# A three-layer kernel on one core: the sigmoids of the opening, the decoding of weight parts, and fill products rearranged

## The chip, the cores and the metric

The kernel runs on one NeuronCore of a Trainium2 chip. The metric is the device time of one execution in microseconds; the figure for a kernel is the median of its runs. The core has five engines with queues of their own: TensorE (PE; its weight loads are shown as PEld), VectorE (DVE), ScalarE (ACT), GpSimd (POOL) and SyncE (SP), which here only issues transfers. Each engine takes its instructions strictly in the order in which they were laid down when the kernel was compiled.

## The reference, cut to what matters

Three stages follow one another. The first is a recurrent attention over 768 steps for 2 batches x 8 heads of width 40, with gates i, f and o; the two others are feed-forward layers of 320 to 2048 to 320 with different nonlinearities, over 1536 tokens.

```python
for t in range(S):                                   # first stage, per batch and head
    m_new = np.maximum(f_gate[t] + m, i_gate[t])
    C = exp(f_gate[t] + m - m_new) * C + exp(i_gate[t] - m_new) * outer(v[t], k[t])
    n = exp(f_gate[t] + m - m_new) * n + exp(i_gate[t] - m_new) * k[t]
    y[t] = sigmoid(o_gate[t]) * (C @ q[t]) / max(abs(n @ q[t]), 1.0)
h = x @ w_in;  x = (h - np.tanh(h)) @ w_out          # second stage (layer 1 below)
h = x @ w_in2; x = (h * tanh(softplus(h))) @ w_out2  # third stage (layer 2 below)
```

## The kernel before, in words

**Tokens and weights.** The 1536 tokens are 12 tiles of 128 (`order`: chunk by chunk, both batches of a chunk together). Layer 1 takes them in six blocks of two tiles, layer 2 in three of four. Each layer's weights come as 16 parts (`NF`), each 128 hidden columns with their share of `w_in` and `w_out`. The loaded words are 64-bit numbers.

**Decoding a part** (`conv_w`) turns them into a high and a low 32-bit half: two steps on VectorE (L179, L180), a scaling on ScalarE (L181), another step on VectorE (L182), a copy that rounds to the high half (`copy_r`, L144 on ScalarE, L148 on GpSimd), and two subtractions that give the remainder, the low half (L185, L186). So a part has five steps on VectorE where the remainder is there too. Before, GpSimd does the remainder for parts 0 and 1 of layer 1 (`f < PRE`), and the high copy for the parts of layer 2 that are decoded before that layer begins (`layer and not second`). `load_w` issues the load of the next part; the buffers are three of `rawp` (parts 0 to 2 of layer 1 lie elsewhere), so a load waits until an earlier part is decoded.

**Attention** (`attention(j)`, a generator that is advanced piece by piece) handles one token tile: decay matrix by products and Exp on ScalarE (L300), scores times decay on VectorE (L319), products with the state (`it`, L326) and with the values (`pv`, L337), denominators, multiplication with the sigmoid of the o gate, and the new state. Tiles of chunk 0 need no state from before. `transpose_x` turns a finished token tile (three transposes, a copy on ScalarE, L252, a subtraction on VectorE, L253) into the input x of layer 1.

**The sigmoids.** `session(c0, c1)` runs the sigmoids of these chunks on ScalarE. They need another function table than Exp and Tanh, so each session has two table loads; the second is forced by a dummy Exp on `scr`, which is recorded in `tbl`. Before, there are two sessions: chunks 0 and 1 in the opening, chunks 2 to 5 in block k = 2 of `attend`. `load_o` loads the o gate in three pieces: chunk 0, chunk 1, and the other four (1.28 MB, inside `lead1`).

**Layer 1 and layer 2.** `tiles` lists the work: layer 1 in two phases, parts 0 to 9 over all six blocks, then parts 10 to 15; each tile takes two parts (`mm1`, 16 products of 256 columns; `tile1`, the nonlinearity on ScalarE, VectorE and GpSimd; `mm2`, two tiles later, 12 products of 320 columns). In layer 2 each tile takes one part and four token tiles (`tile2`, with its own table, Mish). `conv_to` and the main loop decide in which tile a part is decoded: `lead1` for layer 1, `lead2` for layer 2. In layer 2 parts are decoded during the first of the three groups of token tiles.

**Order.** `tc.issue_after(x)`, here `with after([...])`, lays an instruction behind x in the queue of x's engine. Within these bounds a planner lays the instructions of each engine in order when the kernel is compiled, by its own estimate of times and by the order in the source. Fill products (`spin`, `fill[0](n)`, `keep(n, x)`) multiply constants into a bank that nobody reads, to keep TensorE at work; `fill.clear()` ends them after the fifth tile.

## Time and profile before

| | us |
|---|---|
| median of three runs | 486.01 |
| lowest, highest | 485.80, 488.79 |
| the profiled execution | 489.08 |
| its span on the core | 487.3 |
| TensorE busy in the span | 464.8 (95%) |
| VectorE, ScalarE, GpSimd busy | 323.5, 277.8, 129.3 |
| mean granted clock of TensorE | 0.965 of full |

The profile shows one execution, 1.8 us longer than its span. Rows of its order of time give start, length, engine, source line, operation, what is written and from what, the shapes, and the count where neighbours are merged. In square brackets stands how long the engine was idle just before, and whose result ended that. A merged row is as long as from its first start to its last end. The ends of matmuls are modelled, and a few of their records can be missing.

### The profile page before, as it was taken

The page shows a single profiled execution, that of the slowest core. Times are in us where ns is not written, and L with a number is a line of the kernel's source. Part 1 is how long each engine was busy: PE and PEld are TensorE (multiplying, and loading weights), DVE is VectorE, ACT ScalarE, POOL GpSimd, SP SyncE. Part 2 cuts the span into 40 slices and gives each one's busy share as a digit, 9 for nine tenths or more (in the row PEclk, how much of TensorE's full clock was granted, in tenths as well). Part 3 has the DMA queues.
Part 4 walks back from the last instruction along what each step waited for, and adds up shares of the span by engine and source line. Part 5 has one row for each costly group of instructions (what it writes and reads, how often), then busy time and mean ns, then how long its engine had stood idle before and what let it go on. Part 6 is the DMA issues. An engine that isn't in the chain of part 4 may idle for free. (4 is left out here: it accounts for less than half of the span.)

```text
span 487.3 us, 8052 instructions
## 1 busy us (share of the span) xinstructions
PE 464.8 (95%) x3107; PEld 421.0 (86%) x3107; DVE 323.5 (66%) x546; ACT 277.8 (57%) x496; POOL 129.3 (27%) x143
## 2 busy tenths in 40 slices
PE   9867999899999999999999889999999999999996
PEld 5645788899999999999998778998899899899895
DVE  6799798669994978757959998779863222122111
ACT  2858346938836667478777666856663333233231
POOL 2733443343735434334442333200000000000000
PEclk9957799859999999999999999999999999999999
DMA  7951563341060421000110111054301000010001
GB/s 255 370 184 63 179 229 94 100 124 65 37 196 10 128 77 59 1 1 2 61 60 1 60 61 60 2 179 165 132 0 55 0 1 2 0 55 0 1 1 54
DMA packets 22886, 38.05 MB, mean 78 GB/s; under 512 B 1504, under 2 KB 17184, under 8 KB 22848
## 3 DMA queue, kind: packets, MB, share of 16 engines
q1 hardware_dynamic: 22848, 37.54, 23.3%
q8 instruction: 24, 0.39, 0.3%
q14 instruction: 14, 0.11, 0.1%
HBM read 35.41 MB, written 1.97 MB: 77 GB/s over the span
## 5 line engine op out<-in xcount | busy, mean ns | idle before, releaser
L491 PE MATMUL h<-xT,w 128*128 128x256 f32 (+1 forms) x1152 | 210.3, 326 | 10.3 <-DVE t L523 4.2
L491 PEld LDWEIGHTS h<-xT,w 128*128 128x128 f32 x1152 | 170.9, 192 | 28.9 <-issue 6.5
L558 PE MATMUL acc<-w,gh 128*128 128x320 f32 x384 | 121.4, 318 | 1.9 <-DVE xo L575 1.8
L559 PE MATMUL acc<-w,gh 128*128 128x320 f32 x384 | 119.6, 313 | 0.0
L560 PE MATMUL acc<-w,gl 128*128 128x320 f32 x384 | 113.9, 313 | 0.0
L510 POOL TENSOR_TENSOR gl<-g,gh 128x512 fp32r<-128x512 f32 x48 | 65.2, 1359 | 95.3 <-ACT gh L144 84.7
L541 DVE TENSOR_TENSOR gl<-g,gh 128x512 fp32r<-128x512 f32 x48 | 33.2, 691 | 86.2 <-ACT g L540 86.0
L558 PEld LDWEIGHTS acc<-w,gh 128*128 128x128 f32 x384 | 73.1, 190 | 6.8 <-issue 3.2
L559 PEld LDWEIGHTS acc<-w,gh 128*128 128x128 f32 x384 | 73.1, 190 | 2.4
L539 ACT ACTIVATE gh<-h 128x512 fp32r<-128x512 f32 x48 | 28.7, 598 | 76.5 <-PE h L491 76.4
L560 PEld LDWEIGHTS acc<-w,gl 128*128 128x128 f32 x384 | 70.7, 190 | 1.2 <-DVE gl L541 0.3
L144 ACT ACTIVATE gh<-g 128x512 fp32r<-128x512 f32 x48 | 30.4, 633 | 27.5 <-DVE g L528 25.0
L528 DVE COPY_PREDICATED g<-u,t 128x512 f32<-128x512 uint32 x48 | 40.5, 849 | 7.1 <-ACT u L527 6.9
L527 ACT ACTIVATE u<-u,bias 128x512 f32<-128x512 f32 x48 | 34.8, 725 | 16.6 <-DVE g L522 16.5
L522 DVE TENSOR_TENSOR g<-u,h 128x512 f32<-128x512 f32 x48 | 32.7, 681 | 16.4 <-ACT u L521 12.2
L181 ACT ACTIVATE raw<-raw 128x704 f32<-128x704 f32 x32 | 27.5, 864 | 18.6 <-DVE raw L180 18.5
L519 ACT ACTIVATE u<-h 128x512 f32<-128x512 f32 x48 | 28.4, 591 | 16.7 <-PE h L491 16.7
L182 DVE SCALAR_TENSOR_TENSOR raw<-raw 128x704 uint32<-128x704 uint32 x32 | 32.2, 1013 | 4.4 <-ACT raw L181 4.3
L523 DVE TENSOR_TENSOR t<-h,t 128x512 f32<-128x512 f32 x48 | 32.8, 683 | 0.0
L180 DVE SCALAR_TENSOR_TENSOR raw<-raw 128x704 uint32<-128x704 uint32 x32 | 31.3, 981 | 0.3
L521 ACT ACTIVATE u<-u 128x512 f32<-128x512 f32 x48 | 30.4, 638 | 0.0
L144 ACT ACTIVATE w<-raw 128x704 fp32r<-128x704 f32 x27 | 23.0, 867 | 12.6 <-DVE raw L182 12.3
(105 smaller groups left out, 518.8 us busy)
## 6 DMA issues: line engine op xcount, KB each, us to landing
raw<-in_w_dram SPq DMA_DIRECT2D x32, 704.0 KB
qk_t<-in_qk_dram SPq DMA_DIRECT2D x12, 512.0 KB
kv_t<-in_kv_dram SPq DMA_DIRECT2D x12, 324.0 KB
out_dram<-xo SPq DMA_DIRECT2D x12, 160.0 KB
xo<-in_og_dram SPq DMA_DIRECT2D x2, 640.0 KB
xo<-in_og_dram SPq DMA_DIRECT2D x2, 320.0 KB
sd<-nr SPq DMA_DIRECT2D x20, 4.0 KB
md<-nr SPq DMA_DIRECT2D x20, 4.0 KB
```

Source lines behind the costliest of these rows:

```text
L144: nc.scalar.activation(out=o, in_=x, func=AF.Copy)
L182: nc.vector.scalar_tensor_tensor(z, in0=z, scalar=3, in1=lo32, op0=ALU.logical_shift_left, op1=ALU.bitwise_or)
L491: y = nc.tensor.matmul(t[:, k * nt:(k + 1) * nt], lhsT=w[:, o:o + P], rhs=x[:, kk, :], start=(n == 0), stop=(n == len(pairs) - 1),)
L510: nc.gpsimd.tensor_tensor(gl, in0=g, in1=gh.bitcast(F32), op=ALU.subtract)
L522: mark[:] = [nc.vector.tensor_tensor(g, in0=u, in1=h, op=ALU.mult)]
L523: nc.vector.tensor_tensor(t, in0=h, in1=t, op=ALU.subtract)
L527: nc.scalar.activation(out=u, in_=u, func=AF.Relu, bias=bias[:, 0:1])
L528: nc.vector.copy_predicated(out=g, mask=u.bitcast(U32), data=t)
L541: nc.vector.tensor_tensor(gl, in0=g, in1=gh.bitcast(F32), op=ALU.subtract)
L558: nc.tensor.matmul(a, lhsT=gh[:, sl], rhs=wh, start=(f in ends_), stop=False)
L559: nc.tensor.matmul(a, lhsT=gh[:, sl], rhs=wl, start=False, stop=False)
L560: nc.tensor.matmul(a, lhsT=gl[:, sl], rhs=wh, start=False, stop=(f + 1 in ends_ or f == NF - 1))
```

## The change

- `session(0, NCH)` in the opening takes the sigmoids of all six chunks; the session in `attend` goes. The third piece of the o gate is loaded in the first series of loads, right behind weight part 1.
- The copies that complete x for chunk 0 are laid behind the sigmoids, the exponential of `rest_t` behind the dummy Exp, weight part 1's decoding behind the sigmoids (`lead1(PRE, sig)`; on ScalarE).
- Weight parts 2 and up to 9 are laid behind the transposes of the first x (`lead1(..., start)`); the gates' last step also behind the high copy of the part before (`cvd`). Tanh of tile i is laid behind the scaling of part 2i + 2, for the first four tiles.
- Part 1's remainder moves from GpSimd to VectorE. All high copies are on ScalarE.
- Fill products follow the products of the first three tiles, not five; four are added behind each of the two transposes of the first x.
- GpSimd's setting of `sd` and `md` is traced before the first decoding, not after the second.
- Layer 2: four parts are decoded before its first tile, every fourth tile of layer 1's second phase (`R2, E2`: 3, 5 to 4, 4); the rest is spread to 6/7 of a part per tile, not 4/5.

```diff
@@ -129,9 +129,9 @@
 
     last, chain, fill, mark, second = [], [], [], [], []
 
-    texp, tbl, dls = [], [], []
-
-    spq = []
+    texp, tbl, dls, sig = [], [], [], []
+
+    spq, cvd = [], []
 
     def after(x):
         e = ExitStack()
@@ -148,8 +148,7 @@
             nc.gpsimd.tensor_scalar(o, in0=x, scalar1=1.0, scalar2=0.0, op0=ALU.mult, op1=ALU.add)
 
 
-    wtile = {}
-    raw = {}
+    wtile, raw, scaled = {}, {}, {}
     ER = 3
     pending_loads = [(l, f) for l in range(2) for f in range(NF)]
 
@@ -178,10 +177,10 @@
 
         nc.vector.tensor_scalar(lo32, in0=lo32, scalar1=29, scalar2=None, op0=ALU.logical_shift_right)
         nc.vector.scalar_tensor_tensor(lo32, in0=z, scalar=0x80000000, in1=lo32, op0=ALU.bitwise_and, op1=ALU.bitwise_or)
-        nc.scalar.activation(out=zf, in_=zf, func=AF.Copy, scale=2.0 ** -111)
+        scaled[layer, f] = nc.scalar.activation(out=zf, in_=zf, func=AF.Copy, scale=2.0 ** -111)
         nc.vector.scalar_tensor_tensor(z, in0=z, scalar=3, in1=lo32, op0=ALU.logical_shift_left, op1=ALU.bitwise_or)
-        copy_r(2 if layer and not second else 0, w[:, 0:WC], zf)
-        eng = nc.gpsimd if layer == 0 and f < PRE else nc.vector
+        cvd[:] = [nc.scalar.activation(out=w[:, 0:WC], in_=zf, func=AF.Copy)]
+        eng = nc.vector if layer or f else nc.gpsimd
         eng.tensor_tensor(w[:, WC:WT], in0=zf[:, 0:REM0], in1=wf[:, 0:REM0], op=ALU.subtract)
         eng.tensor_tensor(w[64:P, REM0:REM1], in0=zf[64:P, REM0:REM1], in1=wf[64:P, REM0:REM1], op=ALU.subtract)
         wtile[layer, f] = w
@@ -353,7 +352,8 @@
         nc.vector.scalar_tensor_tensor(
             x, in0=x, scalar=1 / WS, in1=den.to_broadcast([P, H, D]), op0=ALU.mult, op1=ALU.mult
         )
-        copy_r(0, xo[:, j, DM:3 * P], xo[:, j, 2 * P:DM])
+        with after(() if c else sig):
+            copy_r(0, xo[:, j, DM:3 * P], xo[:, j, 2 * P:DM])
         yield
         if c + 1 < NCH:
             st = at_ps([P, HG, D1], "st")
@@ -445,7 +445,8 @@
             return rest_t
 
         def rest_t():
-            nc.scalar.activation(out=u_t, in_=u_t, func=AF.Exp, scale=-1.0)
+            with after(tbl):
+                nc.scalar.activation(out=u_t, in_=u_t, func=AF.Exp, scale=-1.0)
             u_ps = at_ps([P, NCH, BH], "u_ps")
             for c in range(NCH):
                 nc.tensor.transpose(u_ps[:, c, :], ch(u_t)[:, c, :], ident[0:BH, 0:BH])
@@ -492,7 +493,7 @@
                     t[:, k * nt:(k + 1) * nt], lhsT=w[:, o:o + P], rhs=x[:, kk, :], start=(n == 0),
                     stop=(n == len(pairs) - 1),
                 )
-            if i < F0[1] // NP:
+            if i < 3:
                 keep(3, y)
         hps[i] = t
 
@@ -515,7 +516,8 @@
         n = len(fs) * nt
         h = hps.pop(i)
         u, t, g = (g2.tile([P, MX], F32, tag=nm, name=nm)[:, 0:n] for nm in "utg")
-        with after(tbl):
+
+        with after(tbl + ([scaled[0, fs[-1] + 1]] if i < F0[1] // NP - 1 else [])):
             texp.append(nc.scalar.activation(out=u, in_=h, func=AF.Tanh, scale=G_B))
             texp.append(nc.scalar.activation(out=t, in_=h, func=AF.Tanh))
         nc.scalar.activation(out=u, in_=u, func=AF.Square, scale=G_SA)
@@ -605,7 +607,7 @@
         make_identity(nc, ident)
         rest, first = gates()
         oc = [(0, 1), (1, 2), (2, NCH)]
-        for x in "qkqkOwOw":
+        for x in "qkqkOwOwO":
             if x == "O":
                 load_o(*oc.pop(0))
             elif x == "w":
@@ -627,7 +629,7 @@
 
         def session(c0, c1):
             with after(texp):
-                sig = [sigmoid_o(B * c, B) for c in range(c0, c1)]
+                sig[:] = [sigmoid_o(B * c, B) for c in range(c0, c1)]
             with after(sig):
                 tbl[:] = [nc.scalar.activation(out=scr, in_=bias[:, 0:1], func=AF.Exp)]
 
@@ -641,7 +643,7 @@
 
         go(ga, 4)
         go(gb, 4)
-        session(0, 2)
+        session(0, NCH)
         go(ga)
         go(gb)
         with after(dls):
@@ -655,8 +657,9 @@
         with after(spq):
             loads_to(2 * B, "kv")
         fill[0](4)
-        transpose_x(0, 0, 0)
-        transpose_x(0, 0, 1)
+        for n in range(2):
+            transpose_x(0, 0, n)
+            keep(4, chain[0])
         start = chain[:]
         conv1 = [0]
 
@@ -666,17 +669,8 @@
                     conv_w(0, conv1[0])
                 if conv1[0] >= PRE:
                     load_w()
-                if conv1[0] == PRE + 1:
-                    with after(spq):
-                        load_o(*oc.pop(0))
                 conv1[0] += 1
 
-        spq[:] = kvd
-        lead1(1)
-        rest = rest()
-        rest = rest()
-        rest = rest()
-        lead1(PRE)
 
         with after(dls):
             nc.gpsimd.memset(sd_.bitcast(F32), 0.0)
@@ -688,12 +682,18 @@
                     out=md_, in_=mf, pattern=[[-HG, 2], [-1, HG], [0, L]], base=-o, channel_multiplier=1,
                     compare_op=ALU.not_equal, fill=-1.0,
                 )
+        spq[:] = kvd
+        lead1(1)
+        rest = rest()
+        rest = rest()
+        rest = rest()
+        lead1(PRE, sig)
         at_pools[:] = [(ps_acc, "acc")] * PS[0] + [(ps_at, "at")] * PS[2]
 
 
         def attend():
             for k in range(1, NB):
-                js, n_st = blk[0, k], 0
+                js = blk[0, k]
                 gens = [(n, attention(j)) for n, j in enumerate(js)]
                 if k < NB - 1:
                     new_xT(0, k)
@@ -701,9 +701,6 @@
                 while gens:
                     for n, g in list(gens[:2]):
                         loads_to(js[n] + 2)
-                        n_st += 1
-                        if k == 2 and n_st == 2 * B + 1:
-                            session(2, NCH)
                         if next(g, 0) == 0:
                             gens.remove((n, g))
                             if k < NB - 1:
@@ -751,19 +748,20 @@
         n_ph = [NB * n // NP for n in PH]
 
 
-        CY, R2, E2 = 6, 3, 5
+        CY, R2, E2 = 6, 4, 4
 
         def conv_to(i, bi, f):
             p = max(n for n in range(len(PH)) if F0[n] <= f)
             e = i - sum(n_ph[:p])
             if p == 0 and bi == 0:
-                lead1(min(F0[1], f + PRE + NP))
+                lead1(min(F0[1], f + PRE + NP), start)
             elif p + 1 < len(PH):
                 w = n_ph[0] // NB if p == 0 else 0
                 lead1(F0[p + 1] + -(-PH[p + 1] * min(e - w + CY, n_ph[p] - w) // (n_ph[p] - w)), mark)
             if p and conv1[0] == NF:
                 lead2(min((i - n_ph[0] + 2) // R2, E2))
 
+        start += cvd
         with after(start):
             rest()
         at_pools[:] = [(ps_at, "at")]
@@ -792,7 +790,7 @@
             if l == 0:
                 conv_to(i, bi, f)
             if l == 1 and bi == supers[0][0]:
-                lead2(max(E2 + (4 * f + 4) // 5, f + 2))
+                lead2(max(E2 + (6 * f + 6) // 7, f + 2))
             mm1(i)
             if l == 0:
                 tile1(i)
```

## Rows read from the trace of the kernel before

**Rows 1.** The page, 40 equal slices of 12.18 us: granted clock in tenths; DMA throughput.

```profile
PEclk9957799859999999999999999999999999999999
GB/s 255 370 184 63 179 229 94 100 124 65 37 196 10 128 77 59 1 1 2 61 60 1 60 61 60 2 179 165 132 0 55 0 1 2 0 55 0 1 1 54
```

**Rows 2.** By stretch: length, busy (count) of PE, PEld, DVE, ACT, POOL; clock; DMA.

```profile
20.00:45.70 25.70, 16.73 (x71) 10.09 (x70) 25.05 (x42) 18.15 (x32) 10.29 (x9) 0.76 0.50 183
43.80:54.00 10.20, 9.48 (x39) 8.06 (x39) 7.87 (x11) 4.99 (x9) 8.44 (x9) 0.52 0.51 175
54.00:93.60 39.60, 39.60 (x302) 33.29 (x299) 32.12 (x57) 25.69 (x41) 13.94 (x17) 1.00 0.39 129
95.35:108.20 12.85, 12.85 (x69) 12.54 (x70) 8.32 (x20) 5.84 (x12) 5.71 (x6) 0.50 0.48 139
108.20:264.00 155.80, 155.37 (x1264) 151.97 (x1264) 124.94 (x214) 108.85 (x205) 65.29 (x66) 1.00 0.18 56
264.00:304.00 40.00, 33.92 (x229) 30.96 (x228) 37.67 (x60) 26.61 (x48) 14.64 (x12) 1.00 0.16 55
312.00:360.00 48.00, 47.91 (x269) 42.90 (x268) 41.89 (x69) 31.63 (x52) 0.00 (x0) 1.00 0.35 121
```

**Rows 3.** Order of time, ScalarE, the second session of sigmoids (L226).

```profile
87.16 1.28 ACT L226 ACT_TABLE_LOAD   x1
88.45 2.62 ACT L226 ACTIVATE xo<-xo 128x640 f32<-128x640 f32 x4
...
92.48 0.83 ACT L144 ACTIVATE w<-raw 128x704 fp32r<-128x704 f32 x1
```

**Rows 4.** Order of time, VectorE, just behind it.

```profile
93.34 0.76 DVE L185 TENSOR_TENSOR w<-raw,w 128x576 fp32r<-128x576 f32 x1 [2.02 <-ACT w L144]
...
94.61 1.29 DVE L319 TENSOR_TENSOR Dm<-sc,Dm 128x512 f32<-128x512 f32 x2
```

**Rows 5.** Order of time, TensorE, in the stretch that follows.

```profile
95.35 3.63 PE L337 MATMUL pv<-kv_t,Dm 128*128 128x41 f32 x16 [1.71 <-DVE Dm L319]
...
103.90 2.69 PE L491 MATMUL h<-xT,w 128*128 128x256 f32 x11
```

**Rows 6.** Order of time, TensorE, 60 to 84 us (L598 are fill products).

```profile
60.10 1.98 PE L337 MATMUL pv<-kv_t,Dm 128*128 128x41 f32 x16
...
65.70 0.82 PE L598 MATMUL w_ps<-const-bfloat16-1.0 128*32 128x512 bf16 x3
...
80.57 3.90 PE L491 MATMUL h<-xT,w 128*128 128x256 f32 x32
```

**Rows 7.** Order of time, VectorE, the first x.

```profile
28.16 1.77 DVE L180 SCALAR_TENSOR_TENSOR raw<-raw 128x704 uint32<-128x704 uint32 x1
29.86 0.54 DVE L253 TENSOR_TENSOR xT<-xt,xT 128x384 fp32r<-128x384 f32 x1
```

**Rows 8.** Order of time, ScalarE, the first x.

```profile
21.67 0.26 ACT L144 ACTIVATE xo<-xo 128x64 f32<-128x64 f32 x1
...
26.27 0.48 ACT L252 ACTIVATE xT<-xt 128x384 fp32r<-128x384 f32 x1
```

**Rows 9.** Order of time, TensorE, the largest gap behind tile 1.

```profile
43.15 1.00 PE L491 MATMUL h<-xT,w 128*128 128x256 f32 x4 [2.34 <-ACT w L144]
```

**Rows 10.** By stretch, decoding alone (tile raw): length, busy (count) of DVE, ACT, POOL.

```profile
228.00:304.00 76.00, 28.83 (x31) 4.36 (x5) 4.58 (x5) 1.00 0.14 48
304.00:360.00 56.00, 31.73 (x49) 18.67 (x22) 0.00 (x0) 1.00 0.30 104
```

**Rows 11.** Order of time, VectorE, last decoding steps of parts 8 and 11, layer 2.

```profile
332.15 0.29 DVE L186 TENSOR_TENSOR w<-raw,w 64x128 fp32r<-64x128 f32 x1
...
345.74 0.29 DVE L186 TENSOR_TENSOR w<-raw,w 64x128 fp32r<-64x128 f32 x1
```

**Rows 12.** Order of time, TensorE, first products of parts 8 and 10, layer 2.

```profile
332.55 2.00 PE L491 MATMUL h<-xT,w 128*128 128x512 f32 x8
...
339.76 2.02 PE L491 MATMUL h<-xT,w 128*128 128x512 f32 x8
```

## The prediction

> **What bounds the kernel now.** I read first the forty slices of the profile's page. The line of the granted clock [rows 1] is short of full in the third to fifth slice (24 to 61 us) and in the eighth and ninth (85 to 110). Then I took the table of stretches [rows 2]. In the opening, 20 to 45.7 us, VectorE is busy 25.05 of 25.70 us and TensorE only 16.73: VectorE sets the pace there. From 54 to 93.6, and from 108.2 to 264, TensorE is busy all the time at full clock: every product taken away there, or pulled out of a slow stretch, is time gained. From 43.8 to 54 and from 95.35 to 108.2 it is as busy, but at half clock, the lower of its two levels (1.2 GHz of 2.4). From 264 to 304 it loses 6.1 us (33.92 of 40) while VectorE is busy 37.67 of 40. From 312 on TensorE is again the bound. So the end is set by TensorE's work, plus its idle time, plus what half clock costs. I price each edit by what it does to those three.
>
> **The second session of sigmoids goes away.** ScalarE loads the sigmoid table at 87.16, runs four sigmoids (2.62 us) and loads the other table back; a weight part's copy waits behind it until 92.48, 5.3 us later [rows 3]. VectorE takes its work in order, so the remainder of that part waits 2.02 us, and behind it stand two steps of the masked scores from 94.61 on [rows 4]. TensorE needs those scores: it starts the product at 95.35 after 1.71 us idle [rows 5]. With that the clock falls, and 12.85 us run at half. The same sixteen small products take 3.63 us there [rows 5] against 1.98 at full clock, and 256-column products 2.69/11 = 0.245 us against 3.90/32 = 0.122 [rows 6]. That is a share of 0.50 to 0.55; with 0.53 the stretch would take 6.8 us, so half clock costs 6.0. Together with the gap: **-7.7**. The bounds: -1.7 if the clock falls there for another reason anyway, -7.7 if both go. I take the upper one, because TensorE is without idle for 39.6 us before the gap and for 155 us after it [rows 2], and the rows lead from the gap to ScalarE without a break.
>
> **Twelve fill products go at tiles 3 and 4.** Three take 0.82 us [rows 6], so twelve take 3.3, less the overlap of their ends: **-3**, in a stretch where TensorE has no idle time. Bounds: 0 (if a weight part is late there and the fills only covered the wait) and -3.3. The eight new fills between the transposes of the first x stand where TensorE idles (25.7 - 16.73 = 9 us [rows 2]). I cost them at nothing; without that cover they are 8 x 0.82/3 = 2.2 us.
>
> **The opening.** VectorE's second half of the first x runs at 29.86, although ScalarE gave its first half at 26.27 + 0.48 = 26.75 [rows 7, 8]. Before it stand steps of weight parts 2 and 3; one took 1.77 us beside GpSimd's work. The change puts these behind x, so x can be whole up to 3.1 us sooner. Against it: part 1's remainder comes to VectorE (0.76 us and 0.29 by [rows 4, 11]); ScalarE gets the four sigmoids (2.62 us [rows 3]), and the copies of x, the table load and part 1's scaling are queued behind them; and the sigmoids wait for the rest of the o gate, 1.28 MB. That load was the last of the opening's group on SP; now SP issues it right behind weight part 1, ahead of two qk loads, parts 2 and 3, two kv loads and parts 4 and 5. At the 370 GB/s of the second slice [rows 1] it holds each of these up by about 3.5 us. Part 2 is wanted later than before, so I count that as hidden. VectorE's work in the stage stays almost the same, and it is the bound, so I give all of this **-1**, not -3.1. Bounds: -7 if the 2.34 us gap at 43.15 [rows 9] goes and the half clock behind it (10.2 us x 0.47 = 4.8) with it; +12 from the first rival. GpSimd's fills of sd and md now stand ahead of part 0's remainder; if that waits for them, it falls inside these bounds. The new order of ScalarE's work (Tanh behind the scaling of the next part; the exponential behind the table) costs nothing: for tiles 0 to 3 the trace has that order already, and the exponential's result is first used by attention in chunk 1.
>
> **Four parts of layer 2 ahead, not five.** Between 228 and 304 us VectorE spends 28.83 us in 31 decoding steps, 0.93 each; later, without GpSimd beside it, 31.73 in 49, 0.65 each [rows 10]. A part has five steps, so one part less relieves VectorE by 4.65 us around the stretch where TensorE idles 6.1. I take about half: **-2.5**; bounds 0 and -4.65. The five copies that move from GpSimd to ScalarE are cheap: ScalarE is busy 26.61 of 40 there [rows 2], and each takes it 0.83 us, as in [rows 3]. Cover gone, that is 4 us on ScalarE.
>
> The part is not saved, only moved behind the layer boundary, and there decoding is just in time. Part 8's last step ends at 332.15 + 0.29 = 332.44 [rows 11], and its products begin at 332.55 [rows 12]. With one part less ahead I expect part n to be ready where part n+1 is now: each load waits for a free buffer, and each decoding step for its tile's place in the queues. Then part 10 ends at 346.03, where part 11 does now [rows 11], but is wanted half-way through its products, at 339.76 + 1.0 [rows 12]: 5.3 us late. VectorE has room to catch up, 6 of 48 us [rows 2], so I take **+4**; bounds 0 and +5.3.
>
> **The sum:** -7.7 - 3 - 1 - 2.5 + 4 = -10.2. The profiled execution took 489.08 us, 1.8 of it around the span, and would come to 478.9. The median of the three runs, 486.01, lies 3.1 below it; from there 475.8, rounded to **476**. The bounds add up to 463 and to 502.
>
> **Rivals.** (1) *The sigmoids wait for data: not faster.* ScalarE is in order. If the o gate's rest still lands with the last of the opening's loads (DMA is busy 0.50 of 20 to 45.7 us [rows 2], which in one go ends at 32.9), the sigmoids end at 35.5, the table is back at 36.8, and x, which took 5.1 us from its first copy at 21.67 to 26.75 [rows 8] and then 0.54 on VectorE, is whole at 42.4 and not at 30.4: +12 in place of -1, which gives 489. It ends above the old time once x is whole 9.2 us later than now, at 39.6; a further half-clock stretch (4.8 us) then makes 494. For it: the loads share one queue and the first bytes set everything behind. Against it: this load is now ninth and not last.
>
> (2) *Decoding in layer 2 is fully late and the middle gains nothing*: -7.7 - 3 - 1 + 5.3 = 479.6. For it: [rows 11, 12]. Against it: VectorE's room.
>
> (3) *The clock falls elsewhere.* The schedule is laid anew, and one more gap of 1 to 2 us in the opening or at tiles 3 and 4 opens another half-clock stretch like that at 43.8 [rows 2], 4.8 us, and the fills' 3 us turn into waiting: 476 + 8 = 484. [...] The trace bears it out in part: all three slow stretches follow idle time of TensorE, but it also ran from tile 5's products at 80.57 [rows 6] to 93.6 without a fill and without a gap.
>
> (4) *The gap at 43.15 goes as well*: some 6 us more, 470.
>
> **Chances.** A measurement of this kernel can tell about 1% (4.9 us) from no change: faster is below 481.1, slower above 490.9. The forecast (471 to 480) has 0.42, all of it faster. Rival 4 has 0.10, faster. Rival 2 has 0.15: 0.09 faster, 0.06 same. Rival 3 has 0.17: 0.03 faster, 0.14 same. Rival 1 has 0.16: 0.05 same, 0.11 slower. Faster 0.64, same 0.25, slower 0.11. The range 468 to 488 leaves out about half of rival 4 and most of rival 1, some 0.15.
>
> **What would show it.** Right: only one sigmoid table load, none near 90 us; no gap over 1 us and a full clock from 60 to 260; no fills after tile 2; the last half of the first x on VectorE before 29 us; TensorE's idle time from 264 to 304 under 4.5 us. The +4 would show as TensorE waiting, before products of parts 7 to 12 of layer 2, for the last decoding step. Wrong: ScalarE idle ahead of the sigmoids beyond 20 us (rival 1), or a half-clock stretch after 60 us (rival 3).

## The result and the profile after

The changed kernel takes 492.91 us (median) against 486.64 of the kernel before on the same chip: ratio 1.0125, 95% interval 1.0087 to 1.0163. It is about 6 us slower. One of its four runs took 499.76 us; it counts in the median and not in the ratio. The prediction said 476 us, range 468 to 488: wrong side, and outside the range. The profiled execution took 493.25 us (span 491.3), 4.2 more than the one of before.

The page of the changed kernel, granted clock in 40 slices of 12.28 us:

```profile
span 491.3 us, 8033 instructions
...
PEclk9797997998999999999999999999989999999999
```

The late slow stretch of before (its eighth and ninth slice [rows 1]) is gone. New dents stand in the seventh slice (74 to 86 us), the tenth (111 to 123) and the thirtieth (356 to 368). The mean granted clock rose all the same, from 0.965 to 0.972, while the time got longer.

The table of stretches, changed kernel (length; busy and count of PE, PEld, DVE, ACT, POOL; clock; DMA share; GB/s):

```profile
20.00:45.70 25.70, 17.99 (x105) 10.51 (x105) 22.05 (x39) 20.02 (x35) 6.98 (x7) 0.78 0.46 160
...
54.00:93.60 39.60, 35.63 (x260) 31.41 (x260) 35.57 (x59) 25.85 (x44) 17.76 (x18) 0.91 0.38 119
95.35:108.20 12.85, 12.85 (x115) 12.56 (x114) 12.73 (x22) 6.58 (x12) 7.19 (x8) 1.00 0.67 222
108.20:264.00 155.80, 151.50 (x1211) 146.25 (x1210) 117.64 (x211) 104.43 (x198) 61.85 (x64) 0.99 0.16 49
264.00:304.00 40.00, 35.95 (x244) 33.06 (x243) 36.20 (x57) 29.19 (x53) 12.27 (x10) 1.00 0.16 55
312.00:360.00 48.00, 45.81 (x251) 40.93 (x250) 41.60 (x71) 30.85 (x50) 0.00 (x0) 0.96 0.41 136
```

Beside [rows 2]: from 95.35 to 108.2 TensorE now runs at full clock and does 115 products where it did 69. From 264 to 304 it idles 4.05 us, not 6.1. But from 54 to 93.6, where it had no idle time, it idles 4 us at a clock of 0.91; from 108.2 to 264 it idles 4.3 us; and in layer 2 there are 2.2 idle us and a clock of 0.96. In the opening VectorE idles 3.65 us (25.70 - 22.05) where it idled 0.65.

To see where time is won and lost I worked out a lead. For every instant I added up the TensorE work begun by then (fills left out, every product priced as at full clock, 0.122 us for 256 columns [rows 6]), and took the difference between two kernels. Minus is ahead of the kernel before:

```
us of TensorE work behind before, at      58    88   106   184   244   304   364
the changed kernel                      -2.0  +1.9  -5.0  +1.9  +1.8  -0.8  +4.0
  won or lost in the stretch            -2.0  +3.9  -6.9  +6.9  -0.1  -2.6  +4.8
  predicted for it                        -1    -3  -7.7     0     0  -2.5    +4
```

The sum, +4.0, answers to the difference of the two profiled executions, 4.2. Two stretches went against the forecast: tiles 3 and 4 (58 to 88 us) lost 3.9 in place of winning 3, and 106 to 184 us gave back the 6.9 that had just been won. In TensorE's order of time these are the waits (start, length, engine, line, what; in brackets idle time and releaser):

```profile
68.49 0.73 PE L492 MATMUL h<-xT,w 128*128 128x256 f32 x4 [0.81 <-ACT w L182]
71.16 0.41 PE L560 MATMUL acc<-w,gh 128*128 128x320 f32 x1 [1.94 <-ACT gh L144]
...
73.29 0.80 PE L492 MATMUL h<-xT,w 128*128 128x256 f32 x2 [0.60 <-DVE w L185]
...
111.97 0.41 PE L249 MATMUL xt<-ident,xo 128*128 128x128 f32 x2 [2.11 <-DVE xo L352]
...
354.76 1.48 PE L492 MATMUL h<-xT,w 128*128 128x512 f32 x4 [2.02 <-ACT w L182]
```

Behind the waits from 68 to 73, behind the one at 111.97 and behind the one at 354.76 the clock falls to the half level for 6.8, 3.4 and 3.4 us. The first wait is for part 8 of layer 1's weights. The order of time of VectorE shows how late the parts were. Part 9's last two steps, changed kernel, and then the same in the kernel before:

```profile
78.78 0.75 DVE L184 TENSOR_TENSOR w<-raw,w 128x576 fp32r<-128x576 f32 x1
79.56 1.27 DVE L185 TENSOR_TENSOR w<-raw,w 64x128 fp32r<-64x128 f32 x1
```

```profile
71.28 0.75 DVE L185 TENSOR_TENSOR w<-raw,w 128x576 fp32r<-128x576 f32 x1
72.06 0.29 DVE L186 TENSOR_TENSOR w<-raw,w 64x128 fp32r<-64x128 f32 x1
```

Part 9 ends at 80.83 in place of 72.35, 8.5 us late; parts 6, 7 and 8 end at 60.5, 65.4 and 73.2 in place of 51.4, 63.2 and 68.9. Before, part 9's products started at 73.07, 0.7 us behind it: TensorE, slowed by fills, and VectorE arrived there together.

Where the lateness begins, the opening shows. ScalarE in the changed kernel:

```profile
19.93 2.62 ACT L225 ACTIVATE xo<-xo 128x640 f32<-128x640 f32 x4 [0.31 <-DMA xo<-in_og_dram]
22.56 1.28 ACT L634 ACT_TABLE_LOAD   x1
...
24.74 0.84 ACT L449 ACTIVATE gu<-gu 16x768 f32<-16x768 f32 x1
25.49 0.81 ACT L180 ACTIVATE raw<-raw 128x704 f32<-128x704 f32 x1
```

and VectorE:

```profile
13.26 1.76 DVE L178 TENSOR_SCALAR raw<-raw 128x704 uint32<-128x704 uint32 x1 [2.69 <-DMA raw<-in_w_dram]
15.05 1.65 DVE L179 SCALAR_TENSOR_TENSOR raw<-raw 128x704 uint32<-128x704 uint32 x1
16.63 1.28 DVE L318 TENSOR_TENSOR Dm<-sc,Dm 128x512 f32<-128x512 f32 x2
...
25.62 0.32 DVE L456 TENSOR_TENSOR ue<-ident,gu 16x96 f32<-16x96 f32 x1 [2.07 <-ACT gu L449]
27.12 0.26 DVE L453 COPY uT<-u_ps 128x96 f32<-128x96 f32 x1 [1.19 <-PE u_ps L452]
...
28.31 1.02 DVE L252 TENSOR_TENSOR xT<-xt,xT 128x384 fp32r<-128x384 f32 x2
```

The exponential of the gates stands behind the table load, and L456, which needs it, stands in VectorE's queue ahead of part 1's next step: 3.26 us idle in two waits. Part 1 ends at 30.74 (before 27.49), part 2, laid behind the first x, at 40.6 (33.3). The loads go through three raw buffers: part 3's end (43.5) lets part 6's load start at 44.4, and part 6's end at 60.5 that of part 9 at 60.6. But VectorE didn't wait for these loads: from 27.1 to 76.6 us it has no idle time over 0.15 us. It reached part 9 late because it had other work ahead of it; how much is counted below, under the bound. The first x is whole at 29.33, 1.07 us sooner.

### The profile page after: what moved, and what is told of

The parts are those of the page before. It is cut to its first block, busy times and chain, and to the rows that moved or that the text cites. A ratio compares the mean times of both kernels' runs of the same rounds, so it can differ in the third digit from the quotient of the medians.

```text
span 491.3 us, 8033 instructions
## 1 busy us (share of the span) xinstructions
PE 461.3 (94%) x3103; PEld 416.9 (85%) x3103; DVE 326.3 (66%) x548; ACT 279.5 (57%) x498; POOL 123.2 (25%) x136
## 4 chain that ended last, share of the span: by engine, by line
PE 48%; DVE 25%; issue 10%; DMA 6%; POOL 5%; ACT 4%; SPq 1%; POOLq 0%; ACTq 0%; DVEq 0%
PE h L492 22%; PE acc L560 7%; PE acc L562 6%; PE acc L561 6%; DMA raw<-in_w_dram 6%; POOL gl L511 4%; DVE raw L181 3%; DVE w L184 3%; DVE raw L178 2%; PE pv L336 2%; DVE g L530 2%; DVE raw L179 2%; DVE w L185 2%; DVE t L525 2%; DVE g L524 2%
## 5 line engine op out<-in xcount | busy, mean ns | idle before, releaser
L492 PE MATMUL h<-xT,w 128*128 128x256 f32 (+1 forms) x1152 | 207.4, 323 | 8.1 <-DVE t L525 3.1
L492 PEld LDWEIGHTS h<-xT,w 128*128 128x128 f32 x1152 | 167.9, 190 | 27.7 <-ACT w L182 3.8
L562 PE MATMUL acc<-w,gl 128*128 128x320 f32 x384 | 109.7, 317 | 0.2 <-DVE gl L543 0.2
L530 DVE COPY_PREDICATED g<-u,t 128x512 f32<-128x512 uint32 x48 | 39.3, 825 | 5.7 <-ACT u L529 5.5
L182 ACT ACTIVATE w<-raw 128x704 fp32r<-128x704 f32 x32 | 27.6, 867 | 12.0 <-DVE raw L181 11.9
L181 DVE SCALAR_TENSOR_TENSOR raw<-raw 128x704 uint32<-128x704 uint32 x32 | 32.3, 1015 | 2.9 <-ACT raw L180 2.9
L179 DVE SCALAR_TENSOR_TENSOR raw<-raw 128x704 uint32<-128x704 uint32 x32 | 30.2, 945 | 0.3
```

Source lines behind the costliest of these rows:

```text
L179: nc.vector.scalar_tensor_tensor(lo32, in0=z, scalar=0x80000000, in1=lo32, op0=ALU.bitwise_and, op1=ALU.bitwise_or)
L181: nc.vector.scalar_tensor_tensor(z, in0=z, scalar=3, in1=lo32, op0=ALU.logical_shift_left, op1=ALU.bitwise_or)
L492: y = nc.tensor.matmul(t[:, k * nt:(k + 1) * nt], lhsT=w[:, o:o + P], rhs=x[:, kk, :], start=(n == 0), stop=(n == len(pairs) - 1),)
L530: nc.vector.copy_predicated(out=g, mask=u.bitcast(U32), data=t)
L562: nc.tensor.matmul(a, lhsT=gl[:, sl], rhs=wh, start=False, stop=(f + 1 in ends_ or f == NF - 1))
```

## The experiments

Part 9's end and the idle time at tiles 3 and 4 come from each run's trace, and so do the leads. One caution holds for all: the planner lays all queues anew for every edit. Only three pairs have the same lead, within 0.5 us, up to 244 us, and are clean from there on: four against five parts ahead on the kernel before, on the kernel with three filled tiles, and on the changed kernel.

| kernel | us | ratio to before (95%) |
|---|---|---|
| changed | 492.91 | 1.0125 (1.0087 to 1.0163) |
| e2 changed, five ahead | 489.38 | 1.007 (1.003 to 1.0111) |
| e3 changed, five tiles filled | 488.43 | 1.0028 (1.0 to 1.0057) |
| e4 changed, two sessions | 486.57 | 1.0002 (0.9976 to 1.0028) |
| e6 changed, five filled, five ahead | 485.31 | 0.9952 (0.9929 to 0.9975) |
| e8 changed, sigmoids 2 to 5 left out | 485.36 | 0.9971 (0.9941 to 1.0) |
| e9 changed, third part free | 494.11 | 1.0107 (1.006 to 1.0155) |
| e16 changed, less decoding | 475.95 | 0.9777 (0.9741 to 0.9813) |
| e1 before, second session left out | 485.13 | 0.9963 (0.9939 to 0.9986) |
| e7 before, three tiles filled | 482.24 | 0.9898 (0.9852 to 0.9944) |
| e10 before, one tile filled | 489.07 | 1.0017 (0.9999 to 1.0035) |
| e11 e7 without the second session | 483.08 | 0.9889 (0.9852 to 0.9927) |
| e12 before, four ahead | 483.35 | 0.9894 (0.9854 to 0.9935) |
| e13 e7 with four ahead | 483.50 | 0.9916 (0.9887 to 0.9945) |
| e14 e13, one session, old order | 487.58 | 1.0 (0.9976 to 1.0025) |
| e15 e13, masks early | 488.69 | 1.0034 (1.0012 to 1.0057) |
| e5 before, new opening | 486.93 | 0.9995 (0.9966 to 1.0024) |
| e17 before, less decoding | 480.17 | 0.9845 (0.98 to 0.989) |

Differences between two kernels below are differences of these ratios times 487 us, with the intervals added in squares. e1, e8 and e11 leave out sigmoids, e16 and e17 a decoding step, so what these five compute is not the reference's.

### e1: the second session alone

```diff
                         n_st += 1
-                        if k == 2 and n_st == 2 * B + 1:
-                            session(2, NCH)
```

> The kernel before without its second session: the sigmoids of chunks 2 to 5 and both table loads near 90 us are left out, so those chunks are multiplied by the raw o gate; nothing else is changed. Theory path (the prediction's step): the gap at 93.6 and the half-clock stretch behind it lie on the path, so the time falls by about 7.7, to 479. Theory slack: VectorE and the attention set when the x of the next block is ready, and TensorE's lead is given back while it waits for that x; the time falls by 1 to 3 us, to 484 to 486, and a gap ahead of the transposes of block 2 or 3 (110 to 150 us) takes the place of the one at 93.6.

1.8 us (0.7 to 3.0) in place of 7.7. Stretches of this kernel:

```profile
95.35:108.20 12.85, 12.85 (x114) 12.53 (x112) 12.76 (x23) 8.07 (x14) 8.60 (x9) 1.00 0.39 109
108.20:264.00 155.80, 153.16 (x1231) 147.90 (x1232) 123.36 (x213) 105.11 (x200) 65.52 (x66) 1.00 0.18 54
```

The half clock goes and the lead at 106 us is 7.6 us. Then TensorE idles 2.6 us up to 264 us where it idled 0.4 [rows 2], the longest time (0.96 us) at 144.03, where it waits for the next block's x, and the lead melts to 4.0 at 364 in this execution. The slack theory held in its number and its sign; the path theory holds for the place, not for the time.

### e2, e3, e4, e6: one part of the change taken back

```diff
# e2
-        CY, R2, E2 = 6, 4, 4
+        CY, R2, E2 = 6, 3, 5
-                lead2(max(E2 + (6 * f + 6) // 7, f + 2))
+                lead2(max(E2 + (4 * f + 4) // 5, f + 2))
# e3
-            if i < 3:
+            if i < F0[1] // NP:
                 keep(3, y)
# e4 (the o gate's third piece is loaded inside lead1 again)
-        session(0, NCH)
+        session(0, 2)
+                        if k == 2 and n_st == 2 * B + 1:
+                            session(2, NCH)
```

e6 is e2 and e3 together.

> The changed kernel with the layer 2 schedule of before (every third tile, five parts ahead, 4/5 of a part per tile). Theory just in time: the gap of 2.0 us at 352.8 and the half clock behind it go (-4.2), and VectorE is fuller from 264 to 304 (+2): about 490.7. Rival: the gap before tile 13 is a chance of the new order and not of the one part less; then the middle alone changes and the time rises to about 495.

> The changed kernel with fill products after five tiles instead of three. Theory fills: the gaps at 67.7 to 73.3 and the half clock from 72.4 to 79.2 come from the missing fills; with them back TensorE stays at full clock there, and some 4 us come back: 489. Rival late parts: parts 8 and 9 end 4 to 8 us later than before, so TensorE waits for them with or without fills; the time stays within 1.5 us of 492.9, and the fills stand where the gaps were.

> The changed kernel with the sigmoids and the o gate's load as before (two sessions, the second in block 2), all else as changed. Theory opening: the four sigmoids in the opening hold up part 1 and the exponential that VectorE waits for, so parts 2 to 9 come 2 to 8 us late; without them the lag at tiles 3 and 4 (3.9 us) goes, and since the second session's gain was given back anyway, the time falls to about 489. Rival: the second session costs what the prediction said, and the time rises by 3 to 7 us, to 496 to 500.

> The changed kernel with fills in five tiles and five parts ahead, both as before; the one stretch of sigmoids and the new opening stay. Theory two separate losses: the fills gave 4.5 us and the five parts 3.5 us, together 8 us, so 485 us. Rival (one loss): both repair the same stall in layer 2 and the clock that falls behind it, so together they give no more than the larger, 488 us.

e2: 2.7 us (0 to 5.4) faster than the changed kernel. The lead is the same up to 244 us; between 304 and 364 us e2 loses nothing where the changed kernel loses 4.8, and it has no wait over 0.3 us there. The theory's other half, a fuller middle with five parts ahead, didn't come: from 264 to 304 us e2's TensorE is busy almost as long as the changed kernel's 35.95.

```profile
264.00:304.00 40.00, 35.59 (x245) 33.02 (x244) 36.52 (x59) 28.09 (x50) 11.63 (x9) 1.00 0.17 55
```

What the changed kernel's wait in layer 2 is, its VectorE shows:

```profile
349.00 0.89 DVE L179 SCALAR_TENSOR_TENSOR raw<-raw 128x704 uint32<-128x704 uint32 x1
352.44 0.53 DVE L178 TENSOR_SCALAR raw<-raw 128x704 uint32<-128x704 uint32 x1 [2.55 <-DMA raw<-in_w_dram]
352.88 0.89 DVE L181 SCALAR_TENSOR_TENSOR raw<-raw 128x704 uint32<-128x704 uint32 x1
```

Part 14's first step waits 2.55 us for its data, whose load could only be issued at 346.88, when part 11 gave up its buffer (end 346.82). Part 13's next step stands behind it in the queue, its products start at 354.76, and the half clock follows.

e3: 4.7 us (2.4 to 7.0) faster. The number agrees with the fill theory, its ground doesn't: the half clock behind tiles 3 and 4 is there with the fills too (73.0 to 79.9), and at 88 us e3 is 5.0 behind before where the changed kernel is 1.9 behind. The fills cost 3 us there, as predicted. They come back later: from 106 to 184 us e3 loses 2.3 and the changed kernel 6.9, and in layer 2 1.7 against 4.8. Why they do isn't shown.

e4: 6.0 us (3.8 to 8.2) faster. The four sigmoids and their data cost more in the opening than the session saved.

e6: 8.4 us (6.3 to 10.6) faster; the 2.7 and 4.7 add up.

### e5: the new order of the opening alone

The changed kernel with the edits of e2, e3 and e4 together; what is left of the change is this, beside the order of the masks, Tanh behind the scaling, the exponential behind the table load, part 1's remainder on VectorE and the high copies on ScalarE:

```diff
-        transpose_x(0, 0, 0)
-        transpose_x(0, 0, 1)
+        for n in range(2):
+            transpose_x(0, 0, n)
+            keep(4, chain[0])
...
-        lead1(PRE)
+        lead1(PRE, sig)
...
-                lead1(min(F0[1], f + PRE + NP))
+                lead1(min(F0[1], f + PRE + NP), start)
```

> The changed kernel with three of its parts taken back: the sigmoids in two sessions as before, fills in five tiles as before, five parts decoded ahead as before. What stays is the new order of the opening (the third part's decoding behind the first x, GpSimd's masks earlier, fills between the first transposes). Theory opening lead: with two sessions the changed kernel had done 4.3 us more TensorE work at 58 us than before; nothing later is left that would take it back, so 483 us against 487.5 of before. Rival (slack): the attention steps set the pace behind 100 us and a lead of the opening is waited away there as that of the left-out second session was: 486 to 488 us.

No gain (-0.2 us, -1.7 to +1.2): the rival's number, though the lead is lost sooner than it said. The lead of 4.2 us at 58 us is there, and at 88 us it is 0.8 us of arrears: part 9 ends at 74.59, 2.2 us later than before.

### e7, e10: fills

```diff
-            if i < F0[1] // NP:
+            if i < 3:        # e7;   e10: if i < 1:
                 keep(3, y)
```

> The kernel before with fills in three tiles in place of five and nothing else changed. Path theory (the prediction's): twelve fills of about 0.25 us each go from TensorE's path, 3 us less, 484.5 us. Slack theory: the fills stood where TensorE would have waited for the next part of the weights anyway, so 487 to 488 us, within 1 us of before.

> The kernel before with fills in tile 0 alone. Path theory (all fills of tiles 1 to 4 stand on TensorE's path): twenty-four fills of 0.25 us go, twelve of them beyond the kernel with three filled tiles, so 3 us under its 482.2 us: 479. Rival (the fills of tiles 1 and 2 stand where TensorE waits for the parts that are decoded up to 47 us): 482 to 483 us, as with three.

e7 wins 5.0 us (2.7 to 7.2), more than the predicted 3, because the half clock at 95 us goes as well, with the session in place. In its order of time the session stands at 83.06, and it holds VectorE up as before:

```profile
84.35 2.62 ACT L226 ACTIVATE xo<-xo 128x640 f32<-128x640 f32 x4
...
89.23 0.76 DVE L185 TENSOR_TENSOR w<-raw,w 128x576 fp32r<-128x576 f32 x1 [2.18 <-ACT w L144]
```

The wait is 2.18 us against 2.02 [rows 4], but TensorE has no gap there: the products with the values start at 91.80 behind other products, and the clock stays full. e10 goes too far: 5.8 us (3.4 to 8.2) slower than e7. TensorE waits for the masked scores, the clock falls for 23.9 us, and a second such wait stands inside that stretch:

```profile
51.56 1.16 PE L317 MATMUL sc<-qk_t 64*128 64x128 f32 x8 [1.22 <-DVE Dm L319]
...
56.49 1.72 PE L337 MATMUL pv<-kv_t,Dm 128*128 128x41 f32 x7 [1.32 <-DVE Dm L319]
```

```profile
53.00:76.90 23.90, 21.22 (x116) 19.92 (x116) 21.12 (x40) 9.11 (x16) 6.22 (x7) 0.50 0.60 194
```

So the fills of tiles 1 and 2 are worth their time in this kernel, those of tiles 3 and 4 are not. Both theories of e10 fell, since neither had the clock in it.

### e11: without the second session, once more

The edits of e7 and e1 together.

> The kernel before with fills in three tiles and without the second session of sigmoids (the gates of chunks 2 to 5 are not computed and the output is not the reference's). Path theory (the prediction's): a session on the path costs 7 us wherever it is, so 475 to 477 us. Theory slack: with three filled tiles the clock did not fall around the session any more, and what the session takes is covered by waits of the attention; without it 481 to 482.5 us, under 1 us less.

Against e7 -0.4 us (-3.3 to +2.5): no difference that can be told, so the path theory fell. Where the gap at 93.64 doesn't arise, the second session costs nothing that shows.

### e12, e13: four parts ahead

```diff
# e12: on before; e13: on e7
-CY, R2, E2 = 6, 3, 5
+CY, R2, E2 = 6, 4, 4
-lead2(max(E2 + (4 * f + 4) // 5, f + 2))
+lead2(max(E2 + (6 * f + 6) // 7, f + 2))
```

> The kernel before with four weight parts of layer 2 decoded ahead in place of five, nothing else changed. The prediction's two terms (2.5 us won between 264 and 304 us, 4 us lost in layer 2): 1.5 us more than before, 488.5 us. Rival (the parts come just in time and one late part costs a wait and a clock fall behind it, as in the changed kernel): the loss alone, 490.5 us. Rival (the loss stands only where the transfer of one part is late, which is not so here): 485 us.

> The kernel before with two parts of the change alone: fills in three tiles and four weight parts of layer 2 decoded ahead; opening and sessions as before. Theory opening: these two parts are worth 4.7 and 4.5 us, they work at different places (88 to 106 us, and 264 to 304 us) and add up, so 478 us, beating both kernels; what makes the changed kernel slower is then the opening with its one stretch of sigmoids, which costs some 15 us against this. Rival (the gains don't add: an earlier TensorE meets a late part in layer 2 as in the changed kernel): 482 to 484 us.

e12 wins 5.2 us (3.2 to 7.1), more than any of the three forecasts; the nearest was the last, 485. Its lead is 0.2 us at 244 and 5.5 at 304; layer 2 takes 1.2 back. The stretches of e12:

```profile
264.00:304.00 40.00, 38.11 (x258) 35.39 (x257) 36.26 (x57) 26.34 (x48) 14.04 (x12) 1.00 0.11 37
312.00:360.00 48.00, 47.49 (x263) 42.26 (x263) 40.47 (x67) 29.68 (x48) 0.00 (x0) 1.00 0.39 136
```

TensorE idles 1.9 us in the middle, not 6.1 [rows 2], and in layer 2 no part is late enough to open a gap of more than 0.4 us. e13 is not 10 us faster than before but 4.1 (2.7 to 5.5). It leads by 7.5 us at 304 and by 5.2 at 364. Its last parts end no earlier in proportion (part 15 at 355.19, e12 355.94), so the earlier TensorE waits for them: that rival held. The middle gains only 3.3 here, as e7 alone wins 1.7 there already. Against e7, four parts ahead are worth nothing that can be told (+0.9 us, -1.8 to +3.5).

### e8, e9, e14, e15: what in the opening costs

```diff
# e8, on the changed kernel (no second session; the o gate's third piece loaded as before)
-        session(0, NCH)
+        session(0, 2)
# e9, on the changed kernel
-                lead1(min(F0[1], f + PRE + NP), start)
+                lead1(min(F0[1], f + PRE + NP))
# e14, on e13 (no second session; the o gate's third piece loaded early)
-        session(0, 2)
+        session(0, NCH)
+            with after(tbl):
                 nc.scalar.activation(out=u_t, in_=u_t, func=AF.Exp, scale=-1.0)
# e15, on e4
-                lead1(min(F0[1], f + PRE + NP), start)
+                lead1(min(F0[1], f + PRE + NP))
-        start += cvd
```

> The changed kernel with the sigmoids of chunks 2 to 5 left out altogether (the gates of those chunks are not computed and the output is not the reference's); the opening has the two sigmoids it had before, and there is no second session. Theory sigmoids: what the changed kernel loses comes from the four added sigmoids standing ahead of part 1's scaling in the opening. Without them the opening's lead is about 4 us at 58 us and the second session is gone as well: 484 us or less, 9 us under the changed kernel. Rival (order and waits: the exponential behind the table load, fewer fills, a part less ahead): the sigmoids cost only their own 2.6 us, so 490 us.

> The changed kernel with the third and later weight parts free to be decoded ahead of the first x again, as before; the one stretch of sigmoids, the three filled tiles and the four parts ahead stay. Theory decoding chain: parts pass through three raw buffers, so a late part 2 makes parts 5 and 8 late; the change put part 2 at 40.6 us against 33.3. Freed, part 2 ends near 34 us, part 9 some 4 us earlier than the 80.8 us of the changed kernel, and the time falls by about 4 us to 488.5. Rival (only the sigmoids make the chain late): part 9 stays within 2 us and the time at 491 to 493.

> The kernel with three filled tiles and four parts ahead, and all sigmoids in one stretch of the opening with the o gate loaded for it; the opening's order is otherwise that of before (masks after the first parts, third part free of the first x). The instructions stand with the scaling of parts 0 and 1 ahead of the four added sigmoids. Theory order: the loss comes from the new order, which puts the sigmoids ahead of part 1's scaling and part 2 behind the first x; here parts 6 to 9 come within 2 us of before and the time is 478 to 480 us. Theory sigmoids: four more sigmoids and their wait for data in the opening cost 5 us or more wherever they stand: 483 to 488 us.

> The changed kernel with the sigmoids in two sessions as before and the third part free of the first x as before; masks on GpSimd early and fills between the first transposes as in the change, three tiles filled and four parts ahead. With the two sessions alone the changed kernel took 486.6 us. Theory decoding chain: the third part's place behind the first x makes parts 6 to 9 late by 3 to 6 us; freed they come with those of before and the time is 479 to 481 us. Rival (the masks, beside which VectorE's steps on part 0 took 1.76 and 1.65 us in place of 0.53 and 0.90, and the wait ahead of the first x do it): 485 to 487 us.

e8: 7.5 us (5.2 to 9.8) under the changed kernel, nearer to the first theory's 484 than to the rival's 490; but only 1.4 us under before, although it has neither a second session nor fills at tiles 3 and 4. Parts 6 to 9 end at 57.8, 63.7, 68.2 and 75.8 and TensorE waits 3.71 us for part 9: the sigmoids are the larger part of the loss and not all of it. e8 is also e4 without its second session, so that session is worth 1.5 us there (-0.4 to +3.4).

e14: 4.1 us (2.2 to 5.9) slower than e13. One stretch of sigmoids makes the parts late in the old order too: part 6 ends at 60.6, part 9 at

```profile
78.47 0.74 DVE L186 TENSOR_TENSOR w<-raw,w 64x128 fp32r<-64x128 f32 x1
```

against 71.43 in e13, although the added sigmoids stand behind the scaling of parts 0 and 1. The theory of the order fell; the theory of the sigmoids held. VectorE waits for the gates' exponential here too, longer than in the changed kernel:

```profile
26.50 0.32 DVE L456 TENSOR_TENSOR ue<-ident,gu 16x96 f32<-16x96 f32 x1 [3.40 <-ACT gu L449]
```

The edit also lays that exponential behind the table load, so what the sigmoids cost by themselves and what this place costs can't be told apart.

e15: 5.7 us (4.0 to 7.5) slower than e13, with two sessions, and no faster than e4 (+1.6 us, -0.1 to +3.2), from which it differs by the freed third part and the gates' last step, freed with it. My theory fell here as well, and the time lies above the rival's range too: with the third part free, part 2 comes at 33.7 as before, but part 9 ends at 73.7 and

```profile
71.51 1.23 PE L492 MATMUL h<-xT,w 128*128 128x256 f32 x4 [4.08 <-ACT w L182]
```

e9 agrees as far as it goes: freeing the third part in the changed kernel makes no difference that can be told (-0.9 us, -3.8 to +2.1), though part 2 came only to 37.45 there and part 9 to 78.30. So the third part's place behind the first x is not the cause. What e15 keeps of the new order (masks early, fills between the transposes, Tanh behind the scaling, the exponential behind the table load, part 1's remainder on VectorE) was not taken apart further.

### e16, e17: less decoding

```diff
+        if layer or not 0 < f < 10:
             nc.vector.scalar_tensor_tensor(lo32, in0=z, scalar=0x80000000, in1=lo32, op0=ALU.bitwise_and, op1=ALU.bitwise_or)
```

> The changed kernel without VectorE's second decoding step (the sign, 0.90 us) for parts 1 to 9 of layer 1, so that these weights lose their sign and the output is not the reference's. Theory decoding chain: VectorE's decoding of parts 1 to 9 is what makes tiles 3 and 4 wait; 9 x 0.9 = 8.1 us less on it bring part 9 from 80.8 to about 74 us, the wait and half clock at 70 to 80 us go, and the time falls by 4 us or more to 489 or below. Rival (TensorE's own work or the data from HBM set the pace there): within 1.5 us of the changed kernel's 492.9 us.

> The kernel before without the same step for parts 1 to 9 of layer 1 (output not the reference's). Theory decoding chain: here the parts come about when TensorE, held by the fills of five tiles, asks for them (part 9 ends at 72.35, its product starts at 73.07), so less decoding is worth at most 2 us: 485 to 487 us. Rival (the step is worth as much as in the changed kernel because VectorE sets the pace everywhere): 479 to 481 us.

Nine steps of 0.9 us less on VectorE before tile 4 make the changed kernel 16.9 us faster (14.4 to 19.5) and the kernel before 7.5 (5.3 to 9.7). Part 9's last step in e16:

```profile
66.56 0.29 DVE L186 TENSOR_TENSOR w<-raw,w 64x128 fp32r<-64x128 f32 x1
```

It ends at 66.85, 14 us sooner than in the changed kernel, from 8.1 us of work taken away. The lead is 9.7 us at 106 and 13.6 at 304, and unlike the changed kernel's it stays. Relieved like this, the changed kernel is the faster of the two by 3.3 us (0.5 to 6.1). For the changed kernel the decoding chain is shown to set the pace; for the kernel before my bound of 2 us was too low and the rival's 479 to 481 held, as VectorE paces it too, less sharply. How much of the 16.9 us is the work itself and how much the new lay of the queues can't be told apart.

## Why the prediction was wrong, point by point

**The bound.** The prediction read 54 to 93.6 and 108.2 to 264 us as TensorE's own, since it was busy without idle time. That was the false step behind the others. "Busy" there holds fills; take them or the half clock out, and another limit stands close behind. Up to tile 4 it is VectorE's decoding: 8.1 us less of it made the changed kernel 16.9 us faster (e16). Behind tile 4 it is the x of the next block out of the attention, as the waits at 111.97 and, in e1, at 144.03 show; no run tested that chain by itself. The Trainium skill has a rule that bears on this, "Perfetto Trace Analysis", section "Identifying the Most-Contended Engine": how busy TensorE's matmuls look is no good measure of how close it is to its limit, while for VectorE occupancy is a fair one. The rows agree: up to part 9's end VectorE was busy 52.98 of 59.4 us in the kernel before, and in the changed kernel 62.43 of 67.9:

```profile
13.00:72.40 59.40, 52.98 (x91) 0.83 0.58 200
```

```profile
13.00:80.90 67.90, 62.43 (x100) 0.85 0.56 185
```

that is, 9.4 us more work and 0.9 us less idle time came ahead of part 9, together its 8.5 us. Most of that work is decoding (the same stretches, decoding alone: VectorE, ScalarE, GpSimd):

```profile
13.00:72.40 59.40, 33.79 (x46) 16.90 (x20) 5.65 (x4) 0.83 0.58 200
13.00:80.90 67.90, 40.68 (x48) 17.08 (x20) 2.26 (x2) 0.85 0.56 185
```

Of these 6.9 us more, part 1's remainder is 1.0; the rest, 5 to 6 us, is the same steps taking longer, which the prediction had not counted (see the last section). What remains of the 9.4 is work laid earlier.

**The second session, -7.7.** Its place and local size were right (-6.9 between 88 and 106 us). But it is worth 1.8 us by itself (e1) and nothing that can be told with fewer fills (e11). The lower bound, -1.7, "if the clock falls there for another reason anyway", had the size, by luck: in e1 the clock does not fall there. The kernel before suggests by itself how little its half clock weighs: of its 92 executions with a clock on record, 34 ran at a mean of 0.969 to 0.975 and 58 at 0.961 to 0.968, like the profiled one. The first had some 6 us less at half clock, 2 x 0.006 x 487, and a median of 485.98 us against 487.94, 2 us less. The lead was given back from 106 to 184 us: the x of block 2 comes at 111.97 in the changed kernel, where before it came at 111.6, so TensorE just arrived early and waited 2.11 us, and the clock fell behind that wait.

**Twelve fills, -3.** Right on the kernel before (e7, -5.0 with the clock that it brings along), wrong in this change, though not at the place: with the fills back TensorE is 3.1 us further behind at 88 us (e3), as forecast, and yet the time is 4.7 us shorter. The gain was lost again later. The loss of 3.9 us from 58 to 88 us is that of the late parts: a weight part was late there, as the bound of 0 had it, with the fills or without.

**The opening, -1.** This is the term with the largest error. x came 1.07 us sooner, as said, and the sigmoids waited 0.31 us for their data, so the first rival's mechanism did not occur. That the exponential behind the table "costs nothing" was false: 2.07 and 1.19 us of idle VectorE, the engine that the prediction itself named as the bound there. The prediction looked at who uses the exponential's result, not at what stands behind its first user in VectorE's queue, which was part 1. The later loads of weights were hidden, as counted. What failed is "VectorE's work in the stage stays almost the same", the ground of the -1: up to part 9 it grew by 9.4 us, and part 9 had been only just in time. Against e13, which has the fills and the four parts ahead of the change, the rest of it, the opening above all, costs 10.2 us (7.8 to 12.5). One stretch of sigmoids in the old order costs 4.1 of it (e14), and the new order with two sessions 4.2 (2.3 to 6.1; e4); together 8.3, so they about add up. On the kernel before that new order cost nothing (e5): what it costs hangs on what else there is to lose.

**Four parts ahead, -2.5 and +4.** In the changed kernel the numbers look nearly exact (-2.6 and +4.8), but the first is luck: e2, with five parts ahead, wins as much in the middle, so that gain comes from something else in the change, which no run isolated (all high copies on ScalarE are one candidate). On the kernel before the same edit is worth -5.2 (e12), since the middle gives 5.3 (more than even the upper bound of 4.65, of which I took half) and layer 2 takes only 1.2. The +4.8 is one late load with a clock fall behind it, and it arose in some of the kernels with four parts ahead and not in others (e3, e4, e12).

**The sum.** It added gains of 7.7, 3 and 2.5 us as if each engine but TensorE had room. e13 shows the limit without any opening: 5.0 and 5.2 make 4.1. The third rival came nearest: one more gap at tiles 3 and 4, a half-clock stretch behind it, the fills turned into waiting. It was priced at 484 because I let the session's gain of 7.7 stand; with the 1.8 of e1 in its place it is 490.

Of the signs set down beforehand, these came: one table load only, no fills behind tile 2, the first x before 29 us on VectorE, 4.05 us idle from 264 to 304, a wait in layer 2 (part 13, not 7 to 12). No gap over 1 us and "a full clock from 60 to 260" did not. A half-clock stretch after 60 us, set down as the sign of rival 3, came.

Four versions that leave nothing out beat both kernels: three filled tiles alone (482.24), four parts ahead alone (483.35) and both (483.50), with no difference between these that can be measured, and e6 (485.31).

## What to carry to other kernels

An engine without idle time need not be the bound if part of its work is filling or slowed by the clock: before pricing a gain there, ask when the next input would have come, and give the gain no more than that. In an opening that one engine paces, price what its queue gains in waits, in work, and in steps that run longer beside another engine, and follow it to the last part that needs it. A gain won early must be followed to the end: here 6.9 us were won in 18 us and lost in the next 78.

## What the runs showed of the hardware

**VectorE beside GpSimd.** With the masks written on GpSimd at the same time (13.39 to 15.96), part 0's first two steps took 1.76 and 1.65 us, against 0.52 and 0.89 for the same steps of part 1. In the kernel before, where the masks come later, part 0's two steps took

```profile
12.64 0.53 DVE L179 TENSOR_SCALAR raw<-raw 128x704 uint32<-128x704 uint32 x1 [1.39 <-DMA raw<-in_w_dram]
13.21 0.90 DVE L180 SCALAR_TENSOR_TENSOR raw<-raw 128x704 uint32<-128x704 uint32 x1
```

although GpSimd was at other work beside them (12.79 to 14.70); in e13, where such work also ran beside it, the first of the two took 1.53. The durations of the remainder's last step up to part 9 (min, median, max in ns), kernel before and changed kernel:

```profile
L186 DVE TENSOR_TENSOR w<-raw,w x8: 288/290/1259, 33.0 to 72.1; 64x128 fp32r<-64x128 f32 x8
```

```profile
L185 DVE TENSOR_TENSOR w<-raw,w x9: 289/670/1269, 30.5 to 79.6; 64x128 fp32r<-64x128 f32 x9
```

The shortest is the same, the median more than doubled. All 16 decoding steps up to part 9 that took over 0.15 us more than the shortest of their line ran beside a GpSimd instruction in the changed kernel, and so did all nine in the kernel before; not every step beside GpSimd is longer. The Trainium skill, "SBUF — State Buffer", section "SBUF: two separate sides", says that the two engines share one pair of ports, which an instruction takes for its whole length while the other engine's blocks; of VectorE's it names those in a two-port mode and, against a GpSimd instruction that reads SBUF, those with two inputs from SBUF. The long durations agree with blocking, but the trace doesn't show which steps take the shared pair, and no run here took GpSimd's work away.

**The clock and gaps.** A wait of 2.18 us in VectorE's queue, behind the session, left the clock at full where TensorE had other products (e7). A gap of 1.22 us was followed by 23.9 us at half (e10), and in e4 one of 0.42 us at 99.3 by 3.4 us at half from 100.2, while e13 had a gap of 1.99 us at 110.4 and kept the full clock: the length of the gap alone doesn't tell. The mean granted clock is no measure of a kernel: the profiled execution of e9 took 491.02 us at 0.984, that of e12 484.77 us at 0.965.
